# Attention and feed-forward kernel, second batch: four product matmuls moved into the wait for q, and the last transposes of q copied by two engines

One Trainium2 chip (trn2), one core. The metric is the time of one execution in microseconds of device time; lower is better.

## The reference

Per batch (8) and head (8), with S = 576 positions, D = 64 and M = 32 memory slots, then a feed-forward layer over C = 512 channels with F = 2048 hidden units:

```python
a = softmax(phi, over m)                       # [S, M]
k_m, v_m = a.T @ k, a.T @ v                    # [M, D] each
attn = softmax(q @ k_m.T / sqrt(D), over m)    # [S, M]
x = (attn @ v_m), heads side by side           # [S, C]
xn = (x - mean) / sqrt(var + 1e-6) * g_ln
out = x + relu(xn @ w_ch1) @ w_ch2
```

All inputs are drawn once from a normal distribution; the output is [8, 576, 512] in float32.

## The kernel before

The program is written by hand in the order in which each engine shall run it. Names in the profile follow the code: `qT` is q transposed, `sc` the scores, `E_sb` their exponentials, `den` the denominators, `Eh` the normalised attention, `w1b` the first weight matrix folded with this batch's v (so that the hidden layer is `Eh @ w1b`), `h_ps` and `rT` the hidden layer before and after the relu, `ch_ps` the product with the second weight matrix (`mm2`), `x_sb` the residual and the output tile. PE is the matmul engine (PEld its weight loads), DVE the vector engine, ACT the scalar engine; POOL and SP here mostly issue DMA, the transfers to and from memory. STT in the prediction is short for DVE's SCALAR_TENSOR_TENSOR. The chain of a profile is the sequence of work that ended last, followed back from the last instruction through what each step waited for.

All matmul results go to PSUM, the memory into which PE writes. The kernel deals out 8 of its banks from two pools: `big` has three buffers of two banks, `one` two of one bank. In this excerpt the comments stand for what is cut:

```python
    def big(shape, dtype, name):
        return psum.tile(shape, dtype, name=name, tag="big", bufs=3)

    def one(shape, dtype, name):
        return psum.tile(shape, dtype, name=name, tag="one", bufs=2)
...
    def a_qT(b, i):              # i: half of the heads; b == 0 and 1 transpose on PE
        ...
        q_ps = big([P, 2, 1024], BF16, "qT_ps")
        for u in range(2):
            for n in range(NP):                       # NP = 5: ten transposes in all
                nc.tensor.transpose(q_ps[:, u, P * n:P * (n + 1)], q_bf[:, 2 * i + u, n, :], ident)
        dst = qTs[b][:, 2 * i:2 * i + 2].rearrange("p a n x -> p a (n x)")
        if i == 0 or b == 1:
            nc.scalar.activation(out=dst, in_=q_ps[:, :, 0:NP * P], func=AF.Copy)
        ...
    def a_sc(b):                 # two groups of scores, each in a big buffer, each followed by an Exp on ACT
    def a_w1b(b, n):             # PE into a big buffer, then a pair of DVE instructions; needs no q
    def mm2(pr, t, j0, j1, ...): # products j0..j1 of output tile t in a `one` buffer; after the 16th, mm2_out
    def mm2_out(pr, t):          # DVE: x = ch_ps * rstd + x, then SP writes x out
...
    mm2(0, 2, 8, 12)
    a_tr(1)
    a_qT(1, 0)
    a_qT(1, 1)
    a_w1b(1, 0)
    mm2(0, 2, 12, 16)
    a_w1b(1, 1)
    a_sc(1)
    mm2(0, 3, 0, 4)
    a_w1b(1, 2)
    a_den(1)
```

Which of the three `big` buffers a tile gets is decided when the program is built; it then carries a wait for the last reader of that buffer.

The softmax here doesn't subtract the row's maximum and nothing guards it: scores larger than these inputs give would overflow.

## Time and profile before

| | before |
|---|---|
| median of the first 3 runs | 253.18 us (253.05 to 253.28) |
| span in the profiled run | 251.4 us |
| PE busy | 236.0 us, 94% |
| first of the last ten transposes | 46.66 us, after 0.91 us of idle PE |
| first h_ps group (start of the hidden layer of batch 1) | 54.68 us in the chain |

The time of a run is about 1.8 us longer than the span in the trace, which starts with the first instruction and ends with the last. Times below that look like 46.66 are microseconds from that start. A time in the chain can lie later than the same work's start in the timeline, because the chain counts an instruction only from where the one before it ends. The stage to look at is the one from the first transposes of batch 1 (45.02) to its first h_ps group: before it, the kernel waits for data; after it, PE is busy for 97 to 98% of the time up to the last output.

### The profile page before, as it was taken

The page shows a single profiled execution, that of the slowest core. Times are in us where ns is not written, and L with a number is a line of the kernel's source. Part 1 is how long each engine was busy: PE and PEld are TensorE (multiplying, and loading weights), DVE is VectorE, ACT ScalarE, POOL GpSimd, SP SyncE. Part 2 cuts the span into 40 slices and gives each one's busy share as a digit, 9 for nine tenths or more (in the row PEclk, how much of TensorE's full clock was granted, in tenths as well). Part 3 has the DMA queues.
Part 4 walks back from the last instruction along what each step waited for, and adds up shares of the span by engine and source line. Part 5 has one row for each costly group of instructions (what it writes and reads, how often), then busy time and mean ns, then how long its engine had stood idle before and what let it go on. Part 6 is the DMA issues. An engine that isn't in the chain of part 4 may idle for free.

```text
span 251.4 us, 5829 instructions
## 1 busy us (share of the span) xinstructions
PE 236.0 (94%) x2446; PEld 131.6 (52%) x2477; DVE 155.1 (62%) x300; ACT 130.1 (52%) x219; POOL 60.0 (24%) x99
## 2 busy tenths in 40 slices
PE   7878999899999999999999999999999999999993
PEld 2443555447534665367534674467444764476453
DVE  3236773595397655787479646885679537873641
ACT  3154662677364464837382646655581755465220
POOL 8643231027204502090206302270205010000000
PEclk9999999999999999999999999999999999999999
DMA  7999999999996798739973998539892300303133
GB/s 148 192 206 207 206 257 215 282 212 128 211 193 128 130 256 182 146 53 202 249 147 89 142 252 136 123 43 223 200 188 44 78 8 0 86 16 71 44 81 83
DMA packets 41922, 36.82 MB, mean 146 GB/s; under 512 B 17444, under 2 KB 37160, under 8 KB 41896
## 3 DMA queue, kind: packets, MB, share of 16 engines
q0 software_dynamic: 17248, 19.53, 45.8%
q1 hardware_dynamic: 24488, 16.79, 29.2%
q8 instruction: 19, 0.31, 0.5%
q10 hardware_dynamic: 160, 0.13, 0.2%
q14 instruction: 7, 0.06, 0.1%
HBM read 41.42 MB, written 9.44 MB: 202 GB/s over the span
## 4 chain that ended last, share of the span: by engine, by line
PE 72%; DMA 17%; ACT 5%; DVE 2%; issue 2%; POOL 1%; POOLq 0%
PE ch_ps L459 41%; PE h_ps L390 22%; DMA q_bf<-in_q_dram 7%; DMA w2b<-in_moe_w_ch_dram 6%; ACT E_sb L313 4%; DMA kv_bf<-in_k_dram 3%; PE w1b_ps L369 2%; PE o_ps L420 2%; DVE x_sb L483 2%; PE kv_ps L205 2%; PE last_ps L471 1%; PE sc_ps L308 1%; POOL q_bf L92 1%; ACT rstd L446 1%; ACT rstd L445 0%
## 5 line engine op out<-in xcount | busy, mean ns | idle before, releaser
L459 PE MATMUL ch_ps<-w2b,rT 128*128 128x512 bf16 x531 | 123.4, 379 | 3.9 <-issue 1.7
L459 PEld LDWEIGHTS <-rT 128*128 128x128 bf16 x560 | 52.2, 98 | 64.5 <-issue 7.8
L390 PE MATMUL h_ps<-Eh,w1b 128*128 128x288 bf16 x512 | 66.7, 285 | 0.7 <-ACT rT L396 0.5
L396 ACT ACTIVATE rT<-h_ps 128x576 bf16<-128x576 f32 x88 | 52.5, 648 | 27.4 <-PE h_ps L390 27.3
L390 PEld LDWEIGHTS <-w1b 128*128 128x128 bf16 x512 | 49.6, 97 | 17.2 <-issue 2.0
L373 DVE SCALAR_TENSOR_TENSOR w1b<-m_sb,rsum,w1b_ps 128x512 bf16<-128x512 f32 x64 | 43.8, 743 | 6.4 <-PE w1b_ps L369 3.5
L398 DVE TENSOR_SCALAR rT<-h_ps 128x576 bf16<-128x576 f32 x40 | 30.3, 758 | 26.9 <-PE h_ps L390 26.3
L483 DVE SCALAR_TENSOR_TENSOR x_sb<-ch_ps,rstd,x_sb 128x512 f32<-128x512 f32 x35 | 25.6, 744 | 8.6 <-PE ch_ps L459 6.9
L426 ACT ACTIVATE x_sb<-o_ps 128x1024 f32<-128x1024 f32 (+1 forms) x20 | 17.8, 933 | 18.4 <-PE o_ps L420 18.4
L439 DVE BATCH_NORM_STATS2 bst<-x_sb 128x6 f32<-128x512 f32 x36 | 24.3, 676 | 3.1 <-ACT x_sb L426 3.1
L189 POOL TENSOR_TENSOR es<-e_sb 128x512 f32<-128x512 bf16 x6 | 6.9, 1156 | 68.1 <-ACT e_sb L182 68.1
L313 ACT ACTIVATE E_sb<-sc_ps,rs 128x640 bf16<-128x640 f32 x16 | 11.8, 790 | 19.5 <-PE sc_ps L308 19.5
L276 POOL TENSOR_TENSOR vb<-v,vmask 128x256 bf16<-128x256 bf16 x12 | 7.7, 662 | 57.3 <-DVE rs L232 57.3
L445 ACT ACTIVATE rstd<-mv,eps_sb 128x2 f32<-128x2 f32 (+1 forms) x20 | 5.9, 296 | 27.3 <-DVE mv L440 27.3
L355 DVE SCALAR_TENSOR_TENSOR Eh<-E_sb,rs,rden 128x576 bf16<-128x576 bf16 x16 | 12.4, 816 | 8.1 <-ACT rden L354 8.1
L174 PE MATMUL w_ps<-fill 128*128 128x512 f32 x14 | 9.8, 819 | 1.6 <-DVE fill L119 1.6
L369 PE MATMUL w1b_ps<-w1r,kvT 64*32 64x512 bf16 x256 | 10.7, 381 | 0.0
L222 DVE CAST k<-kv_ps 128x256 bf16<-128x256 f32 x7 | 3.0, 424 | 12.5 <-PE kv_ps L205 12.5
L182 ACT ACTIVATE e_sb<-phi_st 128x1152 bf16<-128x1152 f32 x8 | 9.2, 1152 | 2.7 <-DMA phi_st<-in_phi_dram 2.7
L354 ACT ACTIVATE rden<-rden 128x576 f32<-128x576 f32 x16 | 10.0, 673 | 0.1
L261 DVE COPY kvT<-kvT_ps 128x256 bf16<-128x256 bf16 x8 | 2.3, 292 | 12.2 <-PE kvT_ps L259 11.8
L92 POOL DMA_DIRECT2D q_bf<-in_q_dram x10 | 7.6, 761 | 4.6 <-DMA w2b<-in_moe_w_ch_dram 1.9
(73 smaller groups left out, 155.1 us busy)
## 6 DMA issues: line engine op xcount, KB each, us to landing
out_dram<-x_sb SPq DMA_DIRECT2D x70, 128.0 KB, 3.5
kv_bf<-in_k_dram POOLq DMA_DIRECT2D x7, 576.0 KB, 8.8
kv_bf<-in_v_dram POOLq DMA_DIRECT2D x7, 576.0 KB, 12.5
phi_st<-in_phi_dram SPq DMA_DIRECT2D x6, 576.0 KB, 10.5
q_bf<-in_q_dram POOLq DMA_DIRECT2D x6, 576.0 KB, 14.9
w1r<-in_moe_w_ch_dram POOLq DMA_DIRECT2D x4, 512.0 KB, 14.2
w2b<-in_moe_w_ch_dram POOLq DMA_DIRECT2D x4, 512.0 KB, 18.8
q_bf<-in_q_dram POOLq DMA_DIRECT2D x4, 288.0 KB, 12.7
```

The costliest lines, as they stand in the source:

```text
L92: nc.gpsimd.dma_start(out=t.rearrange("p j n x -> p j (n x)")[:, js, 0:NS * D], in_=rows(q, b)[:, js, :])
L313: nc.scalar.activation(out=E_[:, g].rearrange("p (a x) -> p a x", a=2), in_=sc[:, :, 0:HP], func=AF.Exp, scale=s["rs"][:, g:g + 1])
L355: nc.vector.scalar_tensor_tensor(out=Eh[:, g, :], in0=s["E"][:, g, 0:S], scalar=s["rs"][:, g:g + 1], in1=rd[:, g].rearrange("p a x -> p (a ...
L369: nc.tensor.matmul(ps[32 * j:32 * (j + 1), g, :], s["kvT"][r:r + 64, 2, 32 * j:32 * (j + 1)], w1r[r:r + 64, j, fs], start=True, stop=True, ...
L373: nc.vector.scalar_tensor_tensor(out=s["w1b"][:, g, fs], in0=m_sb[:, fs], scalar=s["rsum"][:, g:g + 1], in1=ps[:, g, :], op0=ALU.mult, op1 ...
L390: nc.tensor.matmul(h_ps[:, half, 0:HS], s["w1b"][:, g, P * j:P * (j + 1)], s["Eh"][:, g, HS * half:HS * (half + 1)], start=(g == 0), stop= ...
L396: nc.scalar.activation(out=dst, in_=h_ps[:, :, 0:HS], func=AF.Relu)
L398: nc.vector.tensor_scalar(out=dst, in0=h_ps[:, :, 0:HS], scalar1=0.0, scalar2=None, op0=ALU.max)
L426: nc.scalar.activation(out=x[:, 0:n].rearrange("p i (u y) -> p i u y", u=2), in_=o_ps.rearrange("p u (i y) -> p i u y", i=2)[:, 0:n], func ...
L439: nc.vector.bn_stats(out=stt, in_=x)
L459: nc.tensor.matmul(ch_ps, rT[:, j, P * t:P * (t + 1)], w2b[:, j, :], start=(j == 0), stop=(j == JC - 1))
L483: nc.vector.scalar_tensor_tensor(out=x, in0=ch_ps, scalar=rstd, in1=x, op0=ALU.mult, op1=ALU.add)
```

## The change

PE stands idle before the last ten transposes, because their half of q has not landed. The intent is to do four products there that were due after the transposes, and to bring the copy of these transposes out of PSUM sooner by sharing it between ACT and DVE, each with its own half tile.

```diff
-        q_ps = big([P, 2, 1024], BF16, "qT_ps")
+        split = b == 1 and i == 1
+        if split:
+            qs = [one([P, 1024], BF16, "qT_ps") for _ in range(2)]
+        else:
+            q_ps = big([P, 2, 1024], BF16, "qT_ps")
+            qs = [q_ps[:, u, :] for u in range(2)]
         for u in range(2):
             for n in range(NP):
-                nc.tensor.transpose(q_ps[:, u, P * n:P * (n + 1)], q_bf[:, 2 * i + u, n, :], ident)
+                nc.tensor.transpose(qs[u][:, P * n:P * (n + 1)], q_bf[:, 2 * i + u, n, :], ident)
         dst = ...
-        if i == 0 or b == 1:
+        if split:
+            nc.scalar.activation(out=dst[:, 0], in_=qs[0][:, 0:NP * P], func=AF.Copy)
+            nc.vector.tensor_copy(out=dst[:, 1], in_=qs[1][:, 0:NP * P])
+        elif i == 0 or b == 1:
...
     a_qT(1, 0)
+    mm2(0, 2, 12, 16)
     a_qT(1, 1)
     a_w1b(1, 0)
-    mm2(0, 2, 12, 16)
     a_w1b(1, 1)
     a_sc(1)
```

## The prediction

> **What bounds the kernel now.** I read the page first (is one engine the bound?), then the chain of work that ended last around the place where the change acts, then the timeline of the same stretch, engine by engine. The page:
>
> ```profile
> span 251.4 us, 5829 instructions
> PE 236.0 (94%) x2446; PEld 131.6 (52%) x2477; DVE 155.1 (62%) x300; ACT 130.1 (52%) x219; POOL 60.0 (24%) x99
> PE 72%; DMA 17%; ACT 5%; DVE 2%; issue 2%; POOL 1%; POOLq 0%
> ```
>
> PE is busy 94% of the span, so a gain can come only from its idle time (251.4 - 236.0 = 15.4 us) or from fewer products. The change removes no product. The DMA share of the chain is all before 46.61 us; from there to the end the chain is PE with short ACT and DVE links, so whatever shifts PE just after 46.61 us should shift the end by as much. The chain there (start, length, what):
>
> ```profile
> 28.45 18.16 DMA q_bf<-in_q_dram
> 46.61 0.05 issue
> 46.66 0.73 PE qT_ps L293 x10
> 47.39 0.34 PE w1b_ps L369 x8
> 47.73 0.97 PE ch_ps L459 x4
> 48.70 0.34 PE w1b_ps L369 x8
> 49.04 0.18 PE sc_ps L308 x8
> 49.22 0.04 issue
> 49.27 0.33 PE sc_ps L308 x8
> 49.59 0.16 issue
> 49.75 0.81 PE ch_ps L459 x3
> 50.56 0.34 PE w1b_ps L369 x8
> 50.91 0.74 PE den_ps L326 x4
> ```
>
> The second half of batch 1's q lands at 46.61, and PE's ten transposes follow at once. The four ch_ps products that the change moves are those at 47.73. The timeline shows how long PE sat, and what DVE did:
>
> ```profile
> 46.66 0.73 PE L293 MATMUL qT_ps<-ident,q_bf 128*128 128x128 bf16 x10 [0.91 <-DMA q_bf<-in_q_dram]
> 47.43 1.24 ACT L296 ACTIVATE qT<-qT_ps 128x1280 bf16<-128x1280 bf16 x1 [0.41 <-PE qT_ps L293]
> 47.80 1.41 DVE L373 SCALAR_TENSOR_TENSOR w1b<-m_sb,rsum,w1b_ps 128x512 bf16<-128x512 f32 x2 [2.02 <-PE w1b_ps L369]
> 49.13 0.74 DVE L483 SCALAR_TENSOR_TENSOR x_sb<-ch_ps,rstd,x_sb 128x512 f32<-128x512 f32 x1
> 49.26 0.11 PEld L308 LDWEIGHTS <-kvT 64*32 64x32 bf16 x8 [0.44 <-DVE w1b L373]
> ```
>
> The reader is to see two things. The hole on PE is only 0.91 us (45.75 to 46.66). And the last line: the second group of scores waited for DVE's first w1b pair (done 47.80 + 1.41 = 49.21, scores at 49.27), because it takes over that PSUM buffer. So the start of that DVE pair already times PE from here on; DVE is not idle scenery.
>
> **What the Trainium skill says.** "PSUM — Partial Sum Buffer", section "Engine vs sequencer instructions": the Vector and Scalar queues are strict FIFO and matmuls start and complete in program order. The trace agrees: ready products stood behind the transposes for 0.91 us. It is why the move can fill the hole, and why whatever is put ahead of the w1b pair on DVE delays it. "VectorE: DVE Perf Modes", section "The TRN2 errata": a copy out of PSUM costs VectorE 120 + FD/Accel cycles at 0.96 GHz and ScalarE 172 + FD/Accel at 1.2 GHz. Here a DVE bf16 copy of 1280 elements took 824 ns and one of 256 took 292 (formula with Accel 2: 792 and 258, so 33 low), and ACT's of 1280 took 1237 (formula 1210). For 640 elements I estimate 458 + 33 = 0.49 us on DVE and 677 + 27 = 0.70 us on ACT. "Perfetto Trace Analysis", section "Optimizing Tensor Performance", says that independent groups should rotate through different banks so that the evacuation of one overlaps the next one's matmuls. The new half tiles break this, as follows.
>
> **The change part by part.** The built, unrun program gives the order on each engine, the waits and the PSUM banks.
>
> (a) Four ch_ps products move ahead of the second ten transposes. Alone that fills the hole: the first ten transposes end at 45.75, four products cost 0.97 (chain), so they end at 46.72. A transpose can start about 0.16 before such a group ends (before: kvT_ps at 44.74, products until 44.90), that is at 46.56, so the transposes still start with the data at 46.66. 0.97 leaves the later path: at most -0.97, of which the hole pays 0.91.
>
> (b) The last ten transposes go into two single-bank tiles of the pool of two that also holds ch_ps. The first gets the bank of output tile 1, free since DVE's STT at 41.31 + 0.75 = 42.06. The second gets the bank of exactly the four products just moved; the program has the sixth transpose wait for DVE. That STT starts at 46.72 + 0.04 (PE end to DVE start, from kvT_ps 45.07 to 45.11) = 46.76 and takes 0.74: 47.50. With 0.05 from DVE to PE (49.21 to 49.26) the sixth transpose starts at 47.55. Five take 0.73 - 5 x 0.056 = 0.45 (0.056: ten in 0.73, of which 0.22 is one's latency), so they end at 48.00 where before they ended at 47.39: +0.61. On PE, that is a new gap of about 0.6 us.
>
> (c) The evacuation is split. ACT copies the first half 47.14 to 47.84, done 0.83 earlier than before (48.67). DVE copies the second from 48.04 to 48.53. The first scores need both but stand behind two w1b groups on PE (48.00 + 0.34 + 0.34 = 48.68), so the quicker copy buys little: scores at 48.68 where before they started at about 48.9.
>
> (d) On DVE, the order is now STT of the output, copy, then the w1b pair. The pair starts at about 48.48 (neighbours overlap by 0.05, as 49.13 after 49.21 - 0.08 shows) where before it was 47.80: **+0.68**. The output's STT no longer lies between the w1b pairs, but PE does not wait for the later pairs.
>
> (e) What counts is the second scores group. In the new program it again takes over the first w1b group's buffer (banks 6 and 7), with a wait for DVE. The pair ends at 48.48 + 1.41 = 49.89, so the scores start at 49.95, against 49.27. PE has finished the first scores by 48.68 + 0.34 = 49.0 and stands idle for about 0.9 to 1.0 us: the four products that used to stand between the w1b groups and filled this time are used up. After the scores the order is what it was: products, w1b, denominators. Those started 50.91 - 49.27 = 1.64 us after the second scores; the new start is 51.59: +0.68. Their Ln, Exp and the Eh products hang on that, then the first h_ps group (54.68 before, about 55.36 after).
>
> Sum on PE, as a check: hole filled -0.91, transposes' wait +0.6, scores' wait +1.0 = +0.7. By the DVE route: +0.68. Nothing later in the chain has slack of that kind: h_ps at 54.68 to 63 is PE back to back, and then each batch repeats. The program is otherwise the same (no other order changes on any engine). 253.18 + 0.68 = 253.86; I take 253.8, since the small overlaps were all rounded against the change.
>
> **The rivals.** First, the intended gain: the hole of 0.91 is filled and neither new wait bites. For it: PE is in order, the products are ready, and two engines share the copy. Against it: the bank of the second half and the buffer of the second scores are in the built program. It would give 253.18 - 0.9 = 252.3. Second, a wash: the scores' wait is shorter than I think because DVE gets through the output's STT while PE is still in the hole, or because slack before the first h_ps absorbs it (Eh's second half ended at 54.64, PE came at 54.68: both were just in time, so there is almost none). About 253.2. Third, q lands earlier in a run without a profile: then the hole is smaller and the moved products delay the transposes themselves; with q 0.5 us earlier the before-time keeps its order while the new one starts from 46.6, which adds up to 0.5: 254.3. Fourth, DVE's earlier output write (issued about 2.4 us sooner) could collide with loads; q has landed by then, and nothing in the chain after it is DMA, so nothing.
>
> **Range and chances.** Every term is under 1 us of 253, so a change over 2% (5.06 us) would need something outside this stretch. The three runs of before lie within 0.23 us, and the steps (b) and (e) could each be off by 0.2; I give 253.3 to 254.3. Same 0.98, faster 0.01, slower 0.01. For the sign alone I would say 85% slower, 10% faster.
>
> **What would show it right or wrong.** In the new trace: the hole before the second transposes nearly gone; those transposes in two groups of five with a wait of about 0.6 for x_sb's STT; the DVE copy about 0.49 and the ACT copy about 0.70; the first w1b pair on DVE at about 48.5; the second scores waiting about 1 us for that pair; denominators at about 51.6 and the first h_ps at about 55.4. If the sixth transpose does not wait, or the second scores start before 49.5, the prediction is wrong towards a gain. If the first h_ps comes 0.7 later and the end does not, there is slack later that I did not see.

## The result, and the profile after

| | before | changed |
|---|---|---|
| first comparison, 4 runs each, median | 253.23 us | 254.02 us (253.29 to 254.23) |
| ratio of the fast runs | | 1.0023, 95% interval 0.9998 to 1.0048 |
| second comparison, median | 253.44 us (12 runs) | 254.05 us (6 runs) |
| ratio of the fast runs | | 1.0023, 95% interval 1.0009 to 1.0036 |
| span of the profiled run | 251.4 us | 252.2 us |
| first h_ps group | 54.68 us | 55.41 us |

A ratio here is the mean time of one kernel's fast runs over the mean of the other's fast runs of the same rounds, so it is not quite the ratio of the medians. The changed kernel is slower by about 0.6 us, a quarter of a per cent; a difference under 2% is called "same" here.

The page of the changed kernel, the lines that answer to those of before (span, busy times, chain by engine):

```profile
span 252.2 us, 5829 instructions
PE 237.1 (94%) x2446; PEld 132.2 (52%) x2477; DVE 155.3 (62%) x301; ACT 129.7 (51%) x219; POOL 60.0 (24%) x99
PE 82%; ACT 6%; DVE 4%; DMA 4%; issue 2%; POOL 1%; POOLq 0%
```

DVE runs one copy more (301 instructions against 300), and ACT's copy is half as long. The DMA share of the chain fell from 17% to 4%, because in this run PE no longer waits for q: the hole is full. The chain around the place (start, length, what):

```profile
46.09 0.88 PE ch_ps L468 x4
...
47.00 0.76 DVE x_sb L492
47.76 0.04 issue
47.80 0.44 PE qT_ps L299 x5
48.24 0.39 PE w1b_ps L378 x8
48.63 0.06 issue
48.69 1.41 DVE w1b L382 x2
50.09 0.04 issue
50.14 0.33 PE sc_ps L317 x8
...
51.78 0.60 PE den_ps L335 x4
...
55.41 0.57 PE h_ps L399 x4
```

Where before this stretch of the chain was PE alone, DVE now stands in it twice: with x_sb, the output of the moved products, and with the first w1b pair. The answering line of before for the end of the stretch is this one of its chain:

```profile
54.68 0.50 PE h_ps L390 x4
```

In the timeline of the changed kernel (the bracket is the idle time of the engine before it, and what ended it) the two waits and the copy are:

```profile
46.80 0.44 PE L299 MATMUL qT_ps<-ident,q_bf 128*128 128x128 bf16 x5
47.80 0.44 PE L299 MATMUL qT_ps<-ident,q_bf 128*128 128x128 bf16 x5 [0.56 <-DVE x_sb L492]
48.28 0.49 DVE L303 COPY qT<-qT_ps 128x640 bf16<-128x640 bf16 x1 [0.53 <-PE qT_ps L299]
50.14 0.33 PE L317 MATMUL sc_ps<-qT,kvT 64*32 64x320 bf16 x8 [1.00 <-DVE w1b L382]
```

The idle 0.91 us is gone, and 0.56 and 1.00 us have come in its place. So the gain was made, and given back twice.

One thing about this run has nothing to do with the change. PE reached the first transposes of batch 1 at 45.37 where before it was 45.02, and between about 16.6 and 20 us its granted clock was 0.50 (1.00 in the run of before). The Trainium skill, "TensorE: Matmul & The Clock Gate", section "Part 1: The HAM clock gate (the "warmup" mystery)", describes such a gate: two states, half and full, and a free-running window of 3413 ns of activity. The trace agrees in level and length, and of the other profiles only that of move_only has such a stretch (16.7 to 20.1 us). That the slow stretch is what made PE late is not shown: profiles at full clock reach the same place anywhere between 44.79 (big_tile) and 45.53 (two_big). The start of a run is therefore uncertain by a few tenths of a microsecond, which is the size of the effect sought, and the experiments are better compared by distances inside the stage.

### The profile page after: what moved, and what is told of

Read it like the earlier page. It is cut to its first block, busy times and chain, and to the rows that moved or that the text cites. A ratio compares the mean times of both kernels' runs of the same rounds, so it can differ in the third digit from the quotient of the medians.

```text
span 252.2 us, 5829 instructions
## 1 busy us (share of the span) xinstructions
PE 237.1 (94%) x2446; PEld 132.2 (52%) x2477; DVE 155.3 (62%) x301; ACT 129.7 (51%) x219; POOL 60.0 (24%) x99
## 3 DMA queue, kind: packets, MB, share of 16 engines
HBM read 41.42 MB, written 9.44 MB: 202 GB/s over the span
## 4 chain that ended last, share of the span: by engine, by line
PE 82%; ACT 6%; DVE 4%; DMA 4%; issue 2%; POOL 1%; POOLq 0%
PE ch_ps L468 44%; PE h_ps L399 25%; ACT E_sb L322 4%; DMA kv_bf<-in_v_dram 4%; PE w1b_ps L378 2%; PE o_ps L429 2%; PE kv_ps L205 2%; DVE x_sb L492 2%; DVE w1b L382 2%; PE last_ps L480 1%; PE sc_ps L317 1%; PE m_ps L164 1%; PE w_ps L174 1%; POOL q_bf L92 1%; ACT rT L405 1%
## 5 line engine op out<-in xcount | busy, mean ns | idle before, releaser
L174 PE MATMUL w_ps<-fill 128*128 128x512 f32 x14 | 10.5, 876 | 1.6 <-DVE fill L119 1.6
```

What stands on the lines that cost most here:

```text
L174: nc.tensor.matmul(w_ps, fill[:, 0:P], fill, start=True, stop=True)
```

## The experiments

Three calls, eleven kernels; within a call the kernels shared the runs of before, whose medians were 253.44, 253.16 and 253.33 us. The calls ran on different chips, so a kernel is compared with the runs of before of its own call. This table holds, from the timelines, the distance from the first of the last ten transposes to the first w1b pair on DVE, and to the first h_ps group on PE; the third distance counts to h_ps from the first ten transposes of batch 1, that is from PE's arrival at the stage:

| kernel | to the w1b pair, us | to h_ps, us | arrival to h_ps, us | median, us | ratio (95%) |
|---|---|---|---|---|---|
| before | 1.14 | 7.86 | 9.50 | 253.44 | |
| before_pad | 1.14 | 7.86 | 8.81 | 253.14 | 1.0001 (0.9988 to 1.0013) |
| before_q | 1.15 | 7.86 | 9.44 | 253.68 | 0.9998 (0.9967 to 1.0029) |
| changed, first profile | 1.89 | 8.45 | 9.88 | 254.02 | 1.0023 (0.9998 to 1.0048) |
| after_again | 1.77 | 8.32 | 9.88 | 254.05 | 1.0023 (1.0009 to 1.0036) |
| after_pad | 1.89 | 8.45 | 9.87 | 254.56 | 1.0054 (1.0035 to 1.0073) |
| move_only | 1.13 | 7.70 | 9.12 | 253.48 | 1.0006 (0.9989 to 1.0022) |
| act_both | 1.57 | 8.13 | 9.85 | 253.84 | 1.0018 (1.0003 to 1.0034) |
| big_tile | 1.91 | 8.40 | 10.29 | 255.49 | 1.0059 (1.0033 to 1.0085) |
| two_big | 1.26 | 7.82 | 9.24 | 253.31 | 1.0006 (0.9994 to 1.0018) |
| split_only | 1.79 | 8.50 | 9.56 | 253.83 | 1.0005 (0.9975 to 1.0035) |
| w1b_fill | -0.30 | 6.96 | 8.49 | 253.61 | 0.9996 (0.9979 to 1.0014) |
| w1b_fill_q | -0.30 | 6.96 | 8.49 | 252.44 | 0.9945 (0.991 to 0.998) |

The medians take in slow runs, one of before, one of big_tile and two of w1b_fill; the ratios do not. For example, before, by these lines of its timeline and the transposes at 46.66:

```profile
45.02 0.73 PE L293 MATMUL qT_ps<-ident,q_bf 128*128 128x128 bf16 x10
54.52 1.14 PE L390 MATMUL h_ps<-Eh,w1b 128*128 128x288 bf16 x8
```

47.80 - 46.66 = 1.14, 54.52 - 46.66 = 7.86 and 54.52 - 45.02 = 9.50 (the chain joins this h_ps group at 54.68). In all kernels but the two w1b_fill versions, 6.49 to 6.72 us lie between the first two columns: the start of the w1b pair and h_ps move together. From the first h_ps group to the start of the last output (247.64 in before) it is 193.1 to 193.2 us in every profile but that of w1b_fill (194.4).

The third column shows what the first two hide. With the order and copies of before, h_ps comes 7.86 us after q has let the last transposes start, in all three profiles, whether PE arrived 1.64, 0.95 or 1.58 us ahead of them. In the changed kernel it comes 9.87 or 9.88 us after PE's arrival, in all three profiles, although the last transposes started 1.43, 1.56 and 1.42 us after it. So the change takes q's landing off the path and puts a longer way from PE's arrival in its place. With the arrival of before (45.02) the changed kernel's h_ps would come at 54.90, which is 0.38 later than before; with those of before_pad and before_q, 1.07 and 0.44 later. This is an estimate from six profiles; its mean, 0.63, is near the 0.6 us of the timed runs.

### The changed kernel again

No edit.

> The changed kernel once more, with more rounds, because the first interval (0.9998 to 1.0048) does not settle the sign. My theory (the bank of the second half tile and the wait of the second scores): 0.5 to 0.8 us slower than before, ratio 1.002 to 1.003; in the profile the sixth transpose waits about 0.55 us for x_sb and the second scores wait about 1.0 us for w1b. Rival (the 0.7 us of the first comparison came from a slower start of that run, which had a clock of 0.993): ratio within 0.001 of 1.

Measured: 254.05 against 253.44, ratio 1.0023 with the interval clear of 1. The waits in its profile were 0.42 and 1.00 us, and its clock was 0.999, so the loss is not that of a slow clock. The sixth transpose waited 0.13 less than I expected.

### The move alone

```diff
     a_qT(1, 0)
+    mm2(0, 2, 12, 16)
     a_qT(1, 1)
     a_w1b(1, 0)
-    mm2(0, 2, 12, 16)
     a_w1b(1, 1)
```

> Only the four products are moved; the last ten transposes keep their two-bank tile and the one ACT copy. My theory: the hole before the transposes is filled and no transpose waits, but the gain is given back at once, because the first scores now wait for the 1.24 us copy and the second scores still wait for the first w1b pair, which starts no earlier than before: ratio 1.000 (between 0.999 and 1.001). Rival 1, that the move itself is what costs: 0.5 us slower or more. Rival 2, that the move alone would have brought the gain and the split spoils it: 0.6 to 0.9 us faster.

Measured: ratio 1.0006, not distinguishable from before. The timeline, both groups of scores:

```profile
48.98 0.33 PE L308 MATMUL sc_ps<-qT,kvT 64*32 64x320 bf16 x8 [0.77 <-ACT qT L296]
49.52 0.33 PE L308 MATMUL sc_ps<-qT,kvT 64*32 64x320 bf16 x8 [0.22 <-DVE w1b L373]
```

Nothing holds up the transposes, yet 0.77 + 0.22 = 0.99 us of idle PE has come back at the scores. Within the noise the move costs nothing and brings nothing: the products had been standing in time that PE would otherwise have waited. The second rival falls by the interval. The first falls by the profile (h_ps 7.70 us after the transposes, against 7.86); the interval alone, up to 0.56 us slower, just reaches it.

### Two engines, one tile

The move as above and the two copies, with both halves in one two-bank tile as before:

```diff
+        if b == 1 and i == 1:
+            nc.scalar.activation(out=dst[:, 0], in_=q_ps[:, 0, 0:NP * P], func=AF.Copy)
+            nc.vector.tensor_copy(out=dst[:, 1], in_=q_ps[:, 1, 0:NP * P])
```

> Move and two-engine copy, but both halves stay in one tile of the pool with two banks each, so that no half takes the bank of the products just moved. My theory: the wait of the sixth transpose (0.56 us) is gone, the first w1b pair starts at about the same distance from the transposes as before, ratio 1.000 (0.999 to 1.001). Rival (the DVE copy ahead of the w1b pair is what costs): still 0.4 us slower or more.

Measured: a miss. Its timed runs are slower than the changed kernel's, though three of its fast runs had a granted clock of 0.990 to 0.993 and 255.4 to 255.7 us; the two at 0.998 and 1.0 took 254.26 and 253.79. Its timeline, DVE's copy and the second scores:

```profile
48.19 0.49 DVE L297 COPY qT<-qT_ps 128x640 bf16<-128x640 bf16 x1 [1.02 <-ACT qT L296]
49.97 0.33 PE L311 MATMUL sc_ps<-qT,kvT 64*32 64x320 bf16 x8 [0.91 <-ACT E_sb L316]
```

The two copies of one tile run one after the other, DVE waiting for ACT, and the second scores wait for the Exp of the first, as if both had the same buffer. So this run does not answer its question. It does show what the half tiles in the change are good for, and that a copy that comes late on DVE moves the w1b pair (1.91); h_ps (8.40) was late here by way of the first scores, which waited 0.76 us for that copy, and their Exp.

### Both half copies on ACT

```diff
             nc.scalar.activation(out=dst[:, 0], in_=qs[0][:, 0:NP * P], func=AF.Copy)
-            nc.vector.tensor_copy(out=dst[:, 1], in_=qs[1][:, 0:NP * P])
+            nc.scalar.activation(func=AF.Copy, out=dst[:, 1], in_=qs[1][:, 0:NP * P])
```

> The changed kernel with both half copies on ACT, so that DVE has no copy ahead of the w1b pair, while the half tiles keep their single banks. My theory: the bank wait stays (0.56 us) and the w1b pair starts about 0.1 us sooner than in the changed kernel, so 0.5 to 0.6 us slower than before (ratio 1.002). Rival (the DVE copy is what costs): as fast as before.

Measured: ratio 1.0018, still slower than before with no copy on DVE. The timeline:

```profile
47.32 0.44 PE L299 MATMUL qT_ps<-ident,q_bf 128*128 128x128 bf16 x5 [0.26 <-DVE x_sb L492]
49.63 0.33 PE L317 MATMUL sc_ps<-qT,kvT 64*32 64x320 bf16 x8 [0.77 <-DVE w1b L382]
```

Part of the shorter wait of 0.26 us comes from this run's earlier products (45.45, where the changed kernel's began at 45.93), not from the edit. The DVE copy is thus not the main cost. Counted from PE's arrival, h_ps comes at 9.85 us against 9.88, so here the copy costs 0.03 us; the 1.57 in the table is short because the transposes began 1.72 us after the arrival (1.43 in the first profile of the changed kernel).

### Each half in a buffer of its own that is free

```diff
-            qs = [one([P, 1024], BF16, "qT_ps") for _ in range(2)]
+            qs = [big([P, 1024], BF16, "qT_ps") for _ in range(2)]
```

> As the changed kernel, but each half of the last ten transposes has a tile of its own in the pool of two-bank tiles, so that no half takes the bank of the moved products and the two copies are not ordered one after the other (as they were in big_tile, where DVE's copy waited 1.02 us for ACT's). My theory, that the bank of the products costs about 0.5 us and the DVE copy 0.1 us: no wait of the sixth transpose, the first w1b pair 1.2 us after the first of the last transposes (1.1 before, 1.9 in the changed kernel), the second scores wait for it as before, first h_ps group about level with before or 0.1 later; ratio 0.999 to 1.001. Rival (the copy on DVE is the main cost): 0.4 us slower or more.

Measured: 253.31 against 253.16, ratio 1.0006, upper end 1.0018; to the w1b pair 1.26 where I expected 1.2, to h_ps 7.82 against 7.86. The timeline, transposes and second scores:

```profile
46.95 0.72 PE L299 MATMUL qT_ps<-ident,q_bf 128*128 128x128 bf16 x10
49.66 0.33 PE L317 MATMUL sc_ps<-qT,kvT 64*32 64x320 bf16 x8 [0.94 <-DVE w1b L382]
```

The ten transposes run together again, although the move, the DVE copy and the order on DVE are those of the changed kernel. So the loss lies in the bank that the second half tile takes; from PE's arrival to h_ps it is 9.24 us, 0.64 less than in the changed kernel. (The edit moves the first half tile too, for which PE had not waited, and shifts which `big` buffer later tiles get.) The wait of the scores, 0.94, is still there: by itself it costs nothing against before, it is the filled hole given back.

### Late arrival on PE, before and changed

Both kernels with work that is of no use, put ahead of batch 0's products. The results stay right.

```diff
+    pad_ps = one([P, 512], FP32, "pad_ps")
+    for _ in range(3):
+        nc.tensor.matmul(pad_ps, ident, w1r[:, 0, 0:512], start=True, stop=True)
     mm2(0, 0, 0, 4)
```

> The kernel before with three idle products of 128x512 (0.65 us on PE, result unused) ahead of the products of batch 0. My theory, that PE waits for q in the kernel before, so that the hole swallows what comes late ahead of it: PE enters the hole 0.65 later and the hole shrinks from 0.9 to about 0.25 us, time changed by less than 0.25 us. Rival (q does not bind in most runs without a profile): 0.65 us slower, ratio 1.0025.

> The changed kernel with the same three idle products. My theory: the hole is full, so that nothing swallows them: 0.5 to 0.65 us slower than the changed kernel, that is 1.2 to 1.4 us slower than before, ratio 1.0045 to 1.0055. Rival: as the changed kernel, ratio 1.0025.

Measured: the kernel before took 253.14 against 253.16 without the pad, ratio 1.0001 (0.9988 to 1.0013). Its timeline shows what is left of the hole:

```profile
46.46 0.73 PE L293 MATMUL qT_ps<-ident,q_bf 128*128 128x128 bf16 x10 [0.23 <-DMA q_bf<-in_q_dram]
```

PE came to the stage 0.49 later (45.51) and h_ps stayed 7.86 us behind the last transposes. The rival said 0.65 us slower; the interval ends at 0.33. So on the whole q binds in the runs without a profile too.

The changed kernel took 254.56, ratio 1.0054 (1.0035 to 1.0073), where the unpadded one had 1.0023. That is the expected size, but two of its six runs had a clock of 0.990 and 0.991 (255.64 and 254.75); without them its mean is 254.29, 1.07 above that of before in its call, where after_again's fast runs are 0.57 above theirs. That leaves 0.50 for the pad, from four runs that range from 253.73 to 254.98. Its profile cannot settle it, since PE came to the stage at 45.13, no later than in after_again. That the hole of before swallows lateness is shown; inside the stage the changed kernel has no such hole (the third column of the table), but how much of the pad reaches its timed runs is not settled.

### The split alone

As two_big, with the order of the kernel before.

```diff
     a_qT(1, 0)
-    mm2(0, 2, 12, 16)
     a_qT(1, 1)
     a_w1b(1, 0)
+    mm2(0, 2, 12, 16)
     a_w1b(1, 1)
```

> The order of the kernel before, with the last ten transposes in two tiles of the two-bank pool and their copy split between ACT and DVE. My theory: the copy on DVE holds up the first w1b pair by about 0.05 to 0.1 us, on which the second scores wait, and the earlier end of the q copies buys nothing, because the scores stand behind products and w1b groups: ratio 1.0000 to 1.0006. Rival (the 1.24 us copy on ACT was on the path): up to 0.4 us faster, ratio 0.9985.

Measured: ratio 1.0005, but with an interval of 0.6% that settles nothing. Two runs of before took 255.1 and 255.3 us at a clock of 0.991 and 0.992; without them the split is 0.5 us slower. The profile does better, and is not what I expected:

```profile
47.61 0.41 PE L378 MATMUL w1b_ps<-w1r,kvT 64*32 64x512 bf16 x8 [0.58 <-DVE qT L303]
```

The first w1b group got the buffer of the half that DVE copies, so it waited 0.58 us for that copy, and h_ps came 8.50 us after the transposes, not about 7.9. It is the buffer that makes PE wait for the copy; the copy's 0.49 us is then most of the wait.

### The hole filled with what times the stage

If the start of the first w1b pair is what counts, that group belongs in the hole: it needs k and v but no q. Two of the four products go in as well, two stay behind the transposes. The halves lie in one two-bank buffer and in the single bank that is free.

```diff
-            qs = [one([P, 1024], BF16, "qT_ps") for _ in range(2)]
+            qs = [big([P, 1024], BF16, "qT_ps"), one([P, 1024], BF16, "qT_ps")]
...
     a_qT(1, 0)
-    mm2(0, 2, 12, 16)
+    a_w1b(1, 0)
+    mm2(0, 2, 12, 14)
     a_qT(1, 1)
-    a_w1b(1, 0)
+    mm2(0, 2, 14, 16)
     a_w1b(1, 1)
     a_sc(1)
```

> A version meant to beat both: the hole before q is filled with the first w1b group, which needs no q and on whose DVE pair the second scores wait, and with two of the four products; the halves of the last transposes lie in a two-bank tile and in the single bank that is free. My theory (it is the start of the first w1b pair on DVE that times PE after the hole): the pair starts before q lands, the second scores wait for nothing on DVE, first scores 48.2 where before they started at 49.0, first h_ps 0.5 to 0.9 us earlier than before; ratio 0.997 to 0.998. Rival (any filling of the hole is given back, since the Eh products or ACT set the time of h_ps anyway): ratio 0.9995 or more.

Measured: 253.61, ratio 0.9996, the rival's size but, as it turned out, not its cause; the fast runs were 252.50, 252.74, 253.37 and 253.86, beside two slow ones. The stage did what it should. In the profiled run, the one of 253.86, the time did not; two others came close to what I expected. The timeline of the profiled run, the pair, h_ps, and the scores of the next batch:

```profile
46.64 1.41 DVE L382 SCALAR_TENSOR_TENSOR w1b<-m_sb,rsum,w1b_ps 128x512 bf16<-128x512 f32 x2 [0.34 <-PE w1b_ps L378]
53.90 1.21 PE L399 MATMUL h_ps<-Eh,w1b 128*128 128x288 bf16 x8
70.56 0.47 PE L317 MATMUL sc_ps<-qT,kvT 64*32 64x320 bf16 x16 [1.16 <-DMA qT<-q_bf]
```

The first h_ps group came 0.62 us sooner than before (53.90 against 54.52) although PE had entered the hole 0.39 later (45.41 against 45.02), and 16 us later the scores of batch 2 waited 1.16 us for the DMA that transposes that batch's q. It landed 12.2 us after its issue at 58.18, against 9.3 us in the kernel before, where it was in time with 2.3 us to spare. What slowed it I have not isolated, nor whether the runs of 252.50 and 252.74 had this wait; k and v of batch 3 had been asked for 0.5 us sooner than before (58.45 against 58.92).

### The same, with that DMA out of the way

```diff
-    load(2)
+    phi2 = load_phi(2, nc.gpsimd)
+    q2 = load_q(2)                       # ahead of k and v
+    loaded[2] = (phi2, load_kv(2), q2)
...
+    a_qT(2, 0)                           # the transposing DMA
     a_vb(1)
     mm2_out(0, 3)
-    a_qT(2, 0)
```

> w1b_fill gained 0.8 us at the first h_ps group and lost it in the next batch, where the scores waited 1.16 us for the DMA that transposes q of batch 2. Here that batch's q is loaded ahead of its k and v and its transposing DMA is issued ahead of the last output writes of the stage. My theory: the transpose lands before 66 us, the wait is gone and the 0.8 us reach the end: 252.2 to 252.6, ratio 0.9965 to 0.9975. Rival (DMA is so full up to 58 us that what q gains k and v lose): the wait moves to the kv products of batch 2 and the ratio stays at 0.999 or more.

> The kernel before with only that change of the loads. It has 2.3 us of slack at that transpose (landed about 67.6, scores at 69.9), so my theory: nothing, ratio 0.9995 to 1.0005. If it is faster by itself, the gain of w1b_fill_q is not the filled hole's.

Measured: 252.44 (251.56 to 252.76) against 253.33, every run below every run of before. The ratio of 0.9945 is flattered by two runs of before at 255.1 and 255.3 with a clock of 0.991 and 0.992; by the medians it is 0.9965, 0.9 us. The transpose was issued at 51.67, and no wait for it remains in the profile. The timeline at h_ps:

```profile
54.00 1.21 PE L399 MATMUL h_ps<-Eh,w1b 128*128 128x288 bf16 x8
```

The kernel before with the same loads took 253.68, ratio 0.9998 (0.9967 to 1.0029): no faster by itself (without the two runs of before named above it is 0.35 us slower), so the gain is that of the filled hole, once the next wall was moved. This version beats both kernels.

## Why the prediction was right

By its own steps, against the first profile and after_again:

| step | predicted | first profile | after_again |
|---|---|---|---|
| last transposes start | 46.66 | 46.80 | 46.70 |
| (b) wait of the sixth transpose | about 0.6 | 0.56 | 0.42 |
| (c) copies, ACT and DVE | 0.70, 0.49 | 0.70, 0.49 | 0.70, 0.49 |
| (d) first w1b pair on DVE | 48.48 | 48.69 | 48.47 |
| (e) wait of the second scores | 0.9 to 1.0 | 1.00 | 1.00 |
| denominators | 51.59 | 51.78 | 51.56 |
| time | 253.8 | 254.02 | 254.05 |

Step (a), the filled hole: right. The data were no longer what the transposes waited for in the first profile.

Step (b), the bank of the products just moved: right, and two_big shows that it is the main cost. With it gone, everything else of the change left in place, the distance to the w1b pair fell from 1.77 or 1.89 to 1.26 us and the ratio from 1.0023 to 1.0006. The copies of (c) had the sizes forecast.

Step (d), the copy on DVE ahead of the pair: present but small. In two_big it is what remains, 1.26 against 1.14; between act_both and the changed kernel it is 0.03 us. act_both, which has the bank wait without the copy, still lost.

Step (e), the second scores: right in size. move_only and two_big make its part clearer than I had it: this wait takes back about the 0.91 us of (a) (0.99 and 0.94); what is lost beyond that is the delay of the pair.

The mechanism was right, but that the times of the first profile match so closely is partly luck. PE arrived 0.35 later than in the profile from which the sums were made, so the 0.73 us at h_ps (55.41 against 54.68) are 0.35 of lateness and 0.38 of the change, where 0.68 was forecast. Counted from PE's arrival, in the first profile and after_again, two terms were too long. The sum added the moved products end to end behind the transposes, with the STT 1.74 us after the arrival; measured were 1.63 and 1.64, because products began before the transposes had ended. And from the denominators to h_ps it took the 3.77 us of before, where both profiles have 3.63. A smaller slip is in (d): its own lines give an overlap of 49.21 - 49.13 = 0.08 on DVE, not 0.05.

The rival of a filled hole whose gain stays fell in every kernel that only moved the products. The rival of a wash came true, within the noise, for the move alone and for two_big. The third rival, an earlier q, is real as a source of scatter: over the profiles in which the last transposes waited for q, it let them start between 46.30 (split_only) and 47.11 (before_q). The fourth, the earlier output write, falls: it is issued as early in move_only and two_big (47.97 and 47.99, against 47.84 in the changed kernel and 49.96 before), and neither lost time clear of noise. "Nothing later in the chain has slack" holds for a delay: 0.73 us at h_ps in the first profile were 0.81 at the end (248.45 against 247.64 for the last output). For a gain it would have misled: w1b_fill was stopped by a DMA in the next batch, which the chain of the kernel before did not show because it was in time.

What the prediction did not see is that the hole of before is also a buffer against a late start: it set the loss against one arrival of PE, and the loss depends on it (0.38, 1.07 or 0.44 by the estimate above). Nor did it say that runs of one kernel differ by as much as the change (253.29 to 254.23 in the first four), so the sign took more rounds to settle.

## What to carry to other kernels

Before filling an idle stretch, ask what the filler was doing where it stood: here the four products covered a wait for a DVE pair, and taking them away only uncovered it. Fill a hole with the work on which the next wait depends, here the w1b group, and then look for the next wall, which may be a transfer in the next batch that was just in time. When a tile is added, look in the built program at which buffer it gets and who reads that buffer last: a free buffer made the same split nearly harmless, and the buffer of the work just issued cost about half a microsecond. And measure from an event that the change does not move: the distance from the last transposes hid that the two kernels wait for different things.

## What the Trainium skill lacked or had wrong

- "VectorE: DVE Perf Modes", section "The TRN2 errata": its formulas for a copy out of PSUM give (with Accel 2 on DVE and 1 on ACT) 458 ns on DVE and 677 ns on ACT for 640 bf16 elements; the profile of the changed kernel has 491 and 703, that is 33 and 26 ns more, the same excess as at 1280 elements (32 and 27).
- "DMA: Bandwidth & Descriptors", section "Latency and other measured facts", gives a transposing DMA an effective 261 GB/s with a non-contiguous middle dimension. Here one of 128 x 20 x 128 bf16 elements (0.66 MB) landed 4.9 to 12.2 us after its issue (median 5.4 in the kernel before; the 12.2 is w1b_fill's, among other loads), which is 134 to 54 GB/s from issue to landing, another measure than the page's; the page has no figure for a transpose among other loads.
